# Attention, an ELU layer and a maxout layer on one core: the order of the steps where the second stage hands over to the third and the third to the fourth

## The chip, the cores and the metric

The kernel runs on one core of one Trainium2 chip. The time is the device time of one launch in microseconds (us), the median of three runs. TensorE (PE, with its weight loads as PEld), VectorE (DVE), ScalarE (ACT), GpSimd (POOL) and SyncE (SP, which issues nearly all transfers) each work through their own instruction list in order and wait for each other by semaphores.

## The reference

```python
def reference(q, k, v, w_in, w_out, w1, w2, w3, w_out2):      # names shortened
    x = causal_softmax_attention(q, k, v)      # 2 x 12 heads, 448 tokens, 64 wide
    x = x.transpose(0, 2, 1, 3).reshape(896, 768)
    h = x @ w_in                               # 768 -> 2048
    x = np.where(h > 0, h, np.exp(np.minimum(h, 0)) - 1) @ w_out    # 2048 -> 768, "y" in the kernel
    h = np.maximum(np.maximum(x @ w1, x @ w2), x @ w3)   # 768 -> 768 each
    return h @ w_out2                          # 896 x 768
```

The weights are 64-bit floats, which the kernel turns into 32-bit ones on ScalarE and VectorE. From the second stage on, a product is made of three: each operand is split into a high and a low half, and high x high, high x low and low x high are added up in PSUM.

## The kernel before, in words

**First stage** (to about 99 us): attention, by an order written out by hand, with the first parts of `x @ w_in` in it. **Second stage:** 16 blocks of `x @ w_in` with the ELU, then `g @ w_out` in 24 panels `n` (6 column blocks m, 4 panels each, L700 to L732). The weights of a panel lie in one of three buffers with the tag `ws`, the sums in PSUM banks `py[m, 0]` (512 tokens) and `py[m, 1]` (384). `y_copy(m)` brings them to `y` in SBUF. `y` is kept in two halves of rows (blocks 0 to 2 and 3 to 5) and two halves of tokens `T[0]`, `T[1]`.

**Third stage** (L734 to L1016): the three products `x @ w1, w2, w3` by a scheme with seven products of half-size matrices instead of eight, in nine units n = 0 to 8 (`ITEMS`: column block j, matrix i). The seven left operands are splits of parts and sums of `y`: `a00`, `s3` (made early, in the buffer `x1`), `a01`, `s2`, `s1`, `a11`, `s4` (in the pool `late`, which takes the SBUF of the second stage's `g` tiles). `part(name, k, src)` makes a split: one ScalarE copy and one VectorE subtraction. For each unit the right operands come from a `quad` of weights: `split_first(n)` gives `ws_a` (tag `ws` again), `weight_sums(n)` four sums on VectorE, `split_sums(n)` and `split_last(n)` give `wb`. A call `x1(n)` to `x7(n)` is nine matmuls of 448 columns into one PSUM bank: x1, x6, x7, x4 run on in one bank of kind `bx` (three banks), x2 has one of `bz` (three), x5 and x3 share one of `by` (two). Between them `keep_p`, `keep_u`, `keep_v` copy the running sum out on ScalarE, and the `result...` steps add the copies on VectorE and take the maximum into `h`. The steps stand in the order in which each engine does them (`manual_schedule`): the loop at L956 issues for unit n also x1 and x2 of unit n + 2, and the last two units are written out (L981 to L1016). In the loop `turn_half` turns a half block of `w_out2` from doubles; its load goes into the memory that `y` leaves free.

**Fourth stage** (L1023 to L1140): `h @ w_out2` by the same kind of scheme, on quarters `A[t, k]` of `h` and `Bq[k, n]` of `w_out2`: `quadrant` is one of seven products (27 matmuls of 384 columns into three banks), `rest` the 128 tokens left over. `first` holds the splits for its first product, `token_sums(k)` makes the sums of `h` (in place, and `s3`), `t1` to `t4` those of `w_out2`; `fill` splits 1152 columns a partition into a `slot`, and `p1`, `u`, `v` are running sums in SBUF. The 14 answers of 128 x 384 are added into tiles `o` and sent by SP. The banks go round in the order of `kinds`.

PSUM banks and SBUF buffers are reused in the order in which they are asked for: the first instruction that writes a new tile waits for the last use of the old one there. The eight banks of the second stage become `bx`, `bz` and `by` in the order of their first use; y's last two sums `py[5, 0]` and `py[5, 1]` lie in the first two.

Of the kernel before, what the change touches and what calls it, by code (L numbers as in the profile page):

```python
# [31 lines left out]
def tile_attention_elu_maxout(  # L32
# [28 lines left out]
    def f32(ap):  # L61
        return ap.bitcast(F32)
# [594 lines left out]
    def add(out, x, y, op=ALU.add):  # L657
        nc.vector.tensor_tensor(out, x, y, op)  # L658
# [4 lines left out]
    with tc.manual_schedule():  # L663
# [5 lines left out]
        def part(name, k, src):  # L669
            split(ops[name][:, 0, k], ops[name][:, 1, k], src)  # L670
# [121 lines left out]
        def bank3(kind, n):  # L792
            return ps.tile([P, 512], F32, tag=kind, bufs=BUFS[kind], name=f"{kind}{n}")
# [36 lines left out]
        def result_x(n):  # L830
            o, i = place(n, 1, 0)
            if i == 0:
                copy(o, X.pop(n)[:, :S])
            else:
                add(o, o, X.pop(n)[:, :S], ALU.max)

        split_first(0)
        weight_sums(0)
        split_first(1)
        part("a01", slice(0, 2), y[:, 3:5, T[0]])  # L840
        part("s2", slice(0, 2), y[:, 0:2, T[0]])
        part("s1", slice(0, 2), y[:, 0:2, T[1]])
        part("a11", slice(0, 2), y[:, 3:5, T[1]])
        split_sums(0)
        split_last(0)
        add(y[:, 3:5, T[0]], y[:, 3:5, T[0]], y[:, 0:2, T[0]], ALU.subtract)
        part("s4", slice(0, 2), y[:, 3:5, T[0]])
        y_copy(KD - 1)
        h = late.tile([P, KF2, NT], F32, tag="h", name="h")
        x1(0)  # L850
        x1(1)
        part("a01", 2, y[:, 5, T[0]])
# [5 lines left out]
        x2(0)  # L858
        x2(1)
        part("a11", 2, y[:, 5, T[1]])  # L860
        add(y[:, 5, T[0]], y[:, 5, T[0]], y[:, 2, T[0]], ALU.subtract)
        part("s4", 2, y[:, 5, T[0]])
        result(0, 0, 0, p.pop(0), Z.pop(0))
        result(1, 0, 0, p.pop(1), Z.pop(1))

# [35 lines left out]
        def split_left(k):  # L901
            t = cv.tile([P, 2, K2, P], F32R, tag="c", bufs=2, name=f"left{k}")
            lefts.append(t)
            split(t[:, 0], t[:, 1], h[:, k * K2 : (k + 1) * K2, LEFT])

        def first_tiles():
            for k in range(K2):
                t = cv.tile([P, 2, 2, DMO], F32R, tag="ws", bufs=3, name=f"first{k}")
                first.append(t)

        def first_part(k, x):
            src = (A[0, 0], Bq[0, 0])[x][:, k]
            split(first[k][:, x, 0], first[k][:, x, 1], src)

# [6 lines left out]
        def token_sums(k):  # L921
            s = late.tile([P, S], F32, tag="p", bufs=4, name=f"s3_{k}")[:, :DMO]
            add(s, A[0, 0][:, k], A[1, 0][:, k], ALU.subtract)
            s3.append(s)
            add(A[1, 0][:, k], A[1, 0][:, k], A[1, 1][:, k])
            add(A[0, 0][:, k], A[1, 0][:, k], A[0, 0][:, k], ALU.subtract)

        def last_sums(k):
            add(A[0, 1][:, k], A[0, 1][:, k], A[0, 0][:, k], ALU.subtract)

# [1 line left out]
            product("x6", n, X[n], True)  # L932

        def x5(n):
            Y[n] = bank3("by", n)
            product("x5", n, Y[n], False)

        def x7(n):
# [5 lines left out]
        def x3(n):  # L944
            product("x3", n, Y[n], True)
# [10 lines left out]
        for n in range(NI - 2):  # L956
            x6(n)
            if n > 0:
                result_c01(n - 1)
            if n + 3 < NI:  # L960
                load_quad(n + 3)
            split_first(n + 2)
            x5(n)
            keep_u(n)
            weight_sums(n + 1)
            turn_half()
            x7(n)
# [12 lines left out]

# [6 lines left out]
        split_sums(n + 1)  # L987
        split_last(n + 1)
        x7(n)
        first_tiles()  # L990
        x6(n + 1)
        keep_v(n)
        result_c11(n)
        keep_u(n + 1)
        x4(n)
        for k in range(K2):
            first_part(k, 0)
        result_x(n)
        x3(n)
        for k in range(K2):  # L1000
            first_part(k, 1)
        x7(n + 1)
        result_c01(n)
        keep_v(n + 1)
        x5(n + 1)
        tx = late.tile([P, 3, K2, DMO], F32, tag="wb", bufs=2, name="tx")
        t1, t2, t3 = (tx[:, x] for x in range(3))
        token_sums(0)
        result_c11(n + 1)
        x4(n + 1)  # L1010
        add(t1, Bq[0, 1], Bq[0, 0], ALU.subtract)
        add(t3, Bq[1, 1], Bq[0, 1], ALU.subtract)
        result_x(n + 1)
        x3(n + 1)
        split_left(0)
        token_sums(1)  # L1016
        token_sums(2)
        t = act.tile([P, 2, 2, K2, DMO], F32R, tag="x1", name="slot_x1")
        pair["x7"] = t[:, 0], t[:, 1]
        for k in range(K2):  # L1020
            split(t[:, 0, 0, k], t[:, 0, 1, k], s3[k])

        kinds = ["bz", "bz", "bz", "bx", "bx", "by", "bx", "by"]  # L1023

# [28 lines left out]
        def store(o, row, n):  # L1053
            nc.sync.dma_start(out[row : row + P, n * DMO : (n + 1) * DMO], o)

        def answer(t, tok, n):
            return wk.tile([P, 512], F32, tag=f"mx{n}", name=f"o{tok}_{n}_{t}")[:, :DMO]

        def keep(name):
            t = raw_tile(name, name == "v")  # L1060
            return f32(t.rearrange("p n w -> p (n w)"))[:, : K2 * DMO].rearrange(
                "p (t n) -> p t n", t=K2
            )

        p1, u, v = (keep(x) for x in ("p1", "u", "v"))
        f_a, f_b = (lambda c, k, x=x: first[k][:, x, c] for x in range(2))

        x1 = banks("f1_")
        quadrant(x1, f_a, f_b)
        l1 = bank4("l1")  # L1070
        rest(l1, f_b, 0, True)
        fill(pair["x7"][1], t3)
        result_c01(NI - 1)
        for t in range(K2):
            copy(p1[:, t], x1[t])
        add(t2, Bq[1, 1], t1, ALU.subtract)
        pair["x2"] = slot("a01"), slot("s2")
# [12 lines left out]
        fill(pair["x5"][0], A[1, 0])  # L1090
        fill(pair["x5"][1], t1)
        for t in range(K2):
            o = answer(t, 0, 0)
            add(o, p1[:, t], x2[t])
            store(o, t * P, 0)
        x6 = banks("f6_")
        quadrant(x6, *map(side, pair["x6"]))
        pair["x4"] = pair["x7"]
        fill(pair["x4"][0], A[1, 1])
        o = answer(0, 2, 0)  # L1100
        copy(o, l1)
        store(o, LEFT.start, 0)
        t4 = Bq[1, 0]
        add(t4, t4, t2, ALU.subtract)
        for t in range(K2):
            add(u[:, t], p1[:, t], x6[t])
            add(v[:, t], u[:, t], x7[t])
        fill(pair["x4"][1], t4)
        x5 = banks("f5_")
        quadrant(x5, *map(side, pair["x5"]))  # L1110
        for k in range(K2):
# [2 lines left out]
        fill(pair["x3"][0], A[0, 1])  # L1114
        fill(pair["x3"][1], Bq[1, 1])
        for t in range(K2):
            o = answer(t, 1, 1)
            add(o, v[:, t], x5[t])
            store(o, TOK[1].start + t * P, 1)
            add(u[:, t], u[:, t], x5[t])  # L1120
        x4 = banks("f4_")
        quadrant(x4, *map(side, pair["x4"]))
        b12 = pair["x6"][1]
        fill(b12, Bq[0, 1])
        for t in range(K2):
            o = answer(t, 1, 0)
            add(o, v[:, t], x4[t])
            store(o, TOK[1].start + t * P, 0)
        l2 = bank4("l2")
        rest(l2, side(pair["x3"][1]), 1, True)  # L1130
        x3 = banks("f3_")
        quadrant(x3, *map(side, pair["x3"]))
        rest(l2, side(b12), 0, False)
        for t in range(K2):
            o = answer(t, 0, 1)
            add(o, u[:, t], x3[t])
            store(o, t * P, 1)
        o = answer(0, 2, 1)
        copy(o, l2)
        store(o, LEFT.start, 1)  # L1140


# [34 lines left out]
```

## Time and profile before

| | |
|---|---|
| median of 3 runs | 497.69 us (496.41 to 497.90) |
| profiled execution: time, span | 500.33 us, 498.5 us |
| mean granted TensorE clock | 0.993 of full speed |
| busy share of the span | PE 96%, PEld 84%, DVE 78%, ACT 63%, POOL 10% |
| end of the second stage's last product | 323.9 us |
| third stage's products | 329.75 to 449.1 us |
| fourth stage's products | 449.14 to 493.5 us |

The span is from the first to the last instruction of the profiled execution; its time includes 1.83 us around it. Positions below are us from the span's start. An engine's busy share tells little by itself; what counts is where TensorE stands still, and which work ended that.

### The profile page before, as it was taken

To read this page: it belongs to the slowest core of one execution; us is meant where nothing else is said; L and a number is where in the kernel's file an instruction comes from. 1 tells how busy PE (TensorE), PEld (TensorE's weight loads), DVE (VectorE), ACT (ScalarE), POOL (GpSimd) and SP (SyncE) were. 2 spreads that over 40 slices of the span, in tenths; PEclk is the share of its full clock that TensorE was granted. 3 is DMA by queue.
4 is the path that set the end of the run, shared out by engine and by line. 5 is a ranking of instruction groups with operands and counts; after the bars stand their busy time and mean duration, and the time that the engine had idled before them with its cause. 6 is when DMAs were issued, how large, how long until landed. Compare 5 with 4: busy or idle time off the path is not lost.

```text
span 498.5 us, 7505 instructions
## 1 busy us (share of the span) xinstructions
PE 480.9 (96%) x2677; PEld 418.0 (84%) x2677; DVE 386.9 (78%) x758; ACT 316.1 (63%) x648; POOL 50.5 (10%) x104
## 2 busy tenths in 40 slices
PE   9999999999999999999999999959999999998895
PEld 5776767798999988998899899849999999998795
DVE  3999889679989767767767666768788787689884
ACT  4999899578989867766657555545444443435430
POOL 1664665400000000000000000000000000000000
PEclk9999999999999999999999999979999999999999
DMA  9999310037786554256786676403343430000103
GB/s 187 253 226 200 84 37 2 1 101 251 224 276 202 182 180 141 82 183 218 245 262 210 221 250 227 159 0 128 126 127 124 129 102 27 2 1 1 63 17 142
DMA packets 81509, 69.69 MB, mean 140 GB/s; under 512 B 35136, under 2 KB 75328, under 8 KB 81472
## 3 DMA queue, kind: packets, MB, share of 16 engines
q1 hardware_dynamic: 80544, 68.99, 46.4%
q8 instruction: 21, 0.34, 0.3%
q10 hardware_dynamic: 928, 0.23, 0.2%
q14 instruction: 16, 0.13, 0.1%
HBM read 59.38 MB, written 9.83 MB: 139 GB/s over the span
## 4 chain that ended last, share of the span: by engine, by line
PE 84%; DVE 9%; ACT 3%; POOL 2%; DMA 1%; issue 1%; DVEq 0%; ACTq 0%; POOLq 0%
PE ph L357 23%; PE py L723 22%; PE bx L781 14%; PE by L781 6%; PE s L234 4%; PE te L297 4%; PE bz L781 3%; PE av L322 3%; POOL e L287 2%; ACT e L268 1%; DMA out_dram<-o 1%; DVE h L658 1%; DVE slot_x L138 1%; PE idle L448 1%; PE bzf L1035 1%; PE tk L196 1%
## 5 line engine op out<-in xcount | busy, mean ns | idle before, releaser
L357 PE MATMUL ph<-x,ws_l 128*128 128x512 f32 (+2 forms) x576 | 118.7, 365 | 0.0
L723 PE MATMUL py<-gs,ws_o 128*128 128x512 f32 (+1 forms) x576 | 116.2, 363 | 0.0
L357 PEld LDWEIGHTS ph<-x,ws_l 128*128 128x128 f32 x576 | 103.8, 188 | 12.5 <-issue 1.0
L723 PEld LDWEIGHTS py<-gs,ws_o 128*128 128x128 f32 x576 | 104.3, 188 | 11.7
L287 POOL TENSOR_SCALAR e<-e,r 112x336 f32<-112x336 f32 (+3 forms) x96 | 49.1, 532 | 42.6 <-DVE r L281 41.9
L268 ACT ACTIVATE e<-e,nm 112x448 f32<-112x448 f32 (+3 forms) x96 | 49.7, 528 | 3.3 <-DVE nm L254 3.1
L254 DVE CUSTOM_DVE_ANT_0 e<-s,mask 112x224 f32<-112x224 f32 (+3 forms) x96 | 37.9, 441 | 3.2 <-PE s L234 3.0
L781 PE MATMUL by<-ops_s,wb 128*128 128x448 f32 x162 | 36.4, 368 | 0.0
L137 ACT ACTIVATE ws_o<-c_o 128x512 fp32r<-128x512 f32 x24 | 15.1, 631 | 32.2 <-PE py L723 30.7
L781 PEld LDWEIGHTS by<-ops_s,wb 128*128 128x128 f32 x162 | 30.4, 188 | 3.1
L297 PE MATMUL te<-ident,e 112*112 112x112 f32 x240 | 27.7, 261 | 1.5 <-POOL e L287 1.2
L138 DVE TENSOR_TENSOR ws_o<-c_o,ws_o 128x512 fp32r<-128x512 f32 x24 | 16.6, 691 | 15.8 <-ACT ws_o L137 15.8
L661 ACT ACTIVATE u<-bx 128x448 f32<-128x448 f32 x9 | 4.9, 546 | 36.0 <-PE bx L781 36.0
L297 PEld LDWEIGHTS te<-ident,e 112*112 112x112 f32 x240 | 23.8, 133 | 4.4 <-POOL e L287 2.8
L781 PE MATMUL bx<-ops_a_s,ws_a 128*128 128x448 f32 x81 | 20.2, 401 | 5.8 <-ACT y L661 5.8
L234 PE MATMUL s<-qk 64*112 64x224 f32 (+3 forms) x192 | 24.9, 405 | 0.0
L322 PE MATMUL av<-et,vn 112*64 112x448 f32 (+3 forms) x192 | 24.4, 403 | 0.0
L138 DVE TENSOR_TENSOR gs<-g,gs 128x512 fp32r<-128x512 f32 (+2 forms) x30 | 18.7, 622 | 6.9 <-ACT gs L137 6.7
L99 DVE SCALAR_TENSOR_TENSOR ce<-ce,raw_e 128x768 uint32<-128x768 uint32 x18 | 17.2, 958 | 8.6 <-ACT raw_e L95 8.5
L781 PEld LDWEIGHTS bx<-ops_a_s,ws_a 128*128 128x128 f32 x81 | 16.9, 211 | 8.0 <-ACT y L661 6.2
L99 DVE SCALAR_TENSOR_TENSOR c_o<-c_o,raw_o 128x512 uint32<-128x512 uint32 x24 | 16.6, 692 | 8.8 <-ACT raw_o L95 7.4
L137 ACT ACTIVATE gs<-g 128x512 fp32r<-128x512 f32 (+2 forms) x30 | 17.2, 574 | 8.7 <-DVE g L373 8.7
(167 smaller groups left out, 867.5 us busy)
## 6 DMA issues: line engine op xcount, KB each, us to landing
raw_e<-in_moe_w_dram SPq DMA_DIRECT2D x18, 768.0 KB, 4.9
raw_l<-in_moe_w_in_dram SPq DMA_DIRECT2D x16, 768.0 KB, 4.8
raw_o<-in_moe_w_out_dram SPq DMA_DIRECT2D x24, 512.0 KB, 3.5
turned<-ce SPq DMA_DIRECT2D x18, 384.0 KB, 2.7
quad<-turned SPq DMA_DIRECT2D x18, 384.0 KB, 4.3
wx<-in_moe_w_out_dram SPq DMA_DIRECT2D x12, 384.0 KB, 3.1
qn<-in_q_dram SPq DMA_DIRECT2D x24, 112.0 KB, 3.8
vn<-in_v_dram SPq DMA_DIRECT2D x12, 224.0 KB, 3.7
```

What stands on the lines that cost most here:

```text
L99: nc.vector.scalar_tensor_tensor(r, r, 3, low, ALU.logical_shift_left, ALU.bitwise_or)
L137: nc.scalar.activation(hi, src, AF.Copy)
L138: nc.vector.tensor_tensor(lo, src, f32(hi), ALU.subtract)
L234: nc.tensor.matmul(s[j][:C, o : o + (c + 1) * C], qk[:, a, c * C : (c + 1) * C], qk[:, c2, : (c + 1) * C], start=(w == 0 and n == 0), stop ...
L254: nc.vector.tensor_tensor_reduce(out=e_t[h][:, EOFF[c] : EOFF[c] + (c + 1) * C], in0=ps_now.pop(("s", h, c)), in1=mask[:, (NCH - 1 - c) * ...
L268: nc.scalar.activation(e, e, AF.Exp, bias=nm_t[h][:, c : c + 1], scale=-1.0, accum_out=sm_t[p][:, j, c : c + 1],)
L287: nc.gpsimd.tensor_scalar(e, e, ps_now["r", h][:, c : c + 1], 1.0, ALU.mult, ALU.mult)
L297: nc.tensor.transpose(t[:C, n : n + C], e[:, EOFF[c] + j * C : EOFF[c] + (j + 1) * C], ident[:C, :C],)
L322: nc.tensor.matmul(a[j * D : (j + 1) * D, kc * C : S], vn[:, j * NCH + kc, :], et[j][:, TOFF[kc] : TOFF[kc] + S - kc * C], start=(n == 0), ...
L357: nc.tensor.matmul(ps, w(a, kc), x(c, kc), start=(i == 0), stop=(i == len(seq) - 1))
L723: nc.tensor.matmul(py[m, b][:, : at.stop - at.start], w[:, a, kc * P : (kc + 1) * P], g_sp[hk * HK + kc][:, c, at], start=(hk == 0 and i = ...
L781: nc.tensor.matmul(bank[:, :S], w, side[:, c, k, :], start=(not onto and k == 0 and (a, c) == (0, 0)), stop=(k == K2 - 1 and (a, c) == (1, ...
```

## The change

- **Second to third stage.** `weight_sums(0)` goes ahead of `split_first(0)`, and `split_first(1)` behind the first four `part` steps. The subtraction that forms the operand `s4`, and its split, are no longer made for rows 3 and 4 ahead of `y_copy(5)` and for row 5 behind x2(1), but once for all three rows, behind x2(1). The bank of x5(0), kind `by`, is asked for ahead of the banks of x1.
- **Last three units.** `t1`, four of the six `first_part` steps and `token_sums(0)` move up into the loop's last pass (n = 6), between `result_x(6)` and x3(6). The other two `first_part`, `token_sums(1)`, `t3` and the splits of `s3` move up by some steps each among units 7 and 8. `t1` and `t3` lie in buffers of the tags `raw` and `apart` in place of one tile `tx`, `t2` is made later.
- **Answers.** The 14 answers go round over eight buffers (`mx0`, `p`, `mx1`, `p`: two, four, two) in place of two and two. `t4` and the copy of `l1` move, and the two fills for x4 stand among the `u`, `v` sums in place of around them.

```diff
@@ second to third stage
+        weight_sums(0)
         split_first(0)
-        weight_sums(0)
-        split_first(1)
         part("a01", slice(0, 2), y[:, 3:5, T[0]])
         part("s2", slice(0, 2), y[:, 0:2, T[0]])
         part("s1", slice(0, 2), y[:, 0:2, T[1]])
         part("a11", slice(0, 2), y[:, 3:5, T[1]])
+        split_first(1)
         split_sums(0)
         split_last(0)
-        add(y[:, 3:5, T[0]], y[:, 3:5, T[0]], y[:, 0:2, T[0]], ALU.subtract)
-        part("s4", slice(0, 2), y[:, 3:5, T[0]])
         y_copy(KD - 1)
         h = late.tile([P, KF2, NT], F32, tag="h", name="h")
+        Y[0] = bank3("by", 0)
         x1(0)
         x1(1)
...
         part("a11", 2, y[:, 5, T[1]])
-        add(y[:, 5, T[0]], y[:, 5, T[0]], y[:, 2, T[0]], ALU.subtract)
-        part("s4", 2, y[:, 5, T[0]])
+        add(y[:, 3:6, T[0]], y[:, 3:6, T[0]], y[:, 0:3, T[0]], ALU.subtract)
+        part("s4", slice(0, 3), y[:, 3:6, T[0]])
@@ the loop over units, and the last two units
             result_x(n)
+            if n == NI - 3:
+                t1 = keep("t1")
+                add(t1, Bq[0, 1], Bq[0, 0], ALU.subtract)
+                for k in range(K2 - 1):
+                    first_part(k, 0)
+                    first_part(k, 1)
+                token_sums(0)
             x3(n)
...
         x4(n)
-        for k in range(K2):
-            first_part(k, 0)
+        first_part(K2 - 1, 0)
+        first_part(K2 - 1, 1)
         result_x(n)
         x3(n)
-        for k in range(K2):
-            first_part(k, 1)
+        token_sums(1)
         x7(n + 1)
         result_c01(n)
         keep_v(n + 1)
         x5(n + 1)
-        tx = late.tile([P, 3, K2, DMO], F32, tag="wb", bufs=2, name="tx")
-        t1, t2, t3 = (tx[:, x] for x in range(3))
-        token_sums(0)
+        t3 = keep("t3", True)
+        add(t3, Bq[1, 1], Bq[0, 1], ALU.subtract)
         result_c11(n + 1)
         x4(n + 1)
-        add(t1, Bq[0, 1], Bq[0, 0], ALU.subtract)
-        add(t3, Bq[1, 1], Bq[0, 1], ALU.subtract)
+        t = act.tile([P, 2, 2, K2, DMO], F32R, tag="x1", name="slot_x1")
+        pair["x7"] = t[:, 0], t[:, 1]
+        for k in range(K2 - 1):
+            split(t[:, 0, 0, k], t[:, 0, 1, k], s3[k])
         result_x(n + 1)
         x3(n + 1)
+        token_sums(2)
+        split(t[:, 0, 0, 2], t[:, 0, 1, 2], s3[2])
+        fill(pair["x7"][1], t3)
         split_left(0)
-        token_sums(1)
-        token_sums(2)
-        t = act.tile([P, 2, 2, K2, DMO], F32R, tag="x1", name="slot_x1")
-        pair["x7"] = t[:, 0], t[:, 1]
-        for k in range(K2):
-            split(t[:, 0, 0, k], t[:, 0, 1, k], s3[k])
@@ fourth stage
-        def answer(t, tok, n):
-            return wk.tile([P, 512], F32, tag=f"mx{n}", name=f"o{tok}_{n}_{t}")[:, :DMO]
+        homes = ["mx0", "p", "mx1", "p"]
+        def answer(name):
+            homes.append(homes.pop(0))
+            if homes[-1] == "p":
+                return late.tile([P, S], F32, tag="p", bufs=4, name=name)[:, :DMO]
+            return wk.tile([P, 512], F32, tag=homes[-1], name=name)[:, :DMO]
...
+        t4 = Bq[1, 0]
+        add(t4, t4, t2, ALU.subtract)
         x6 = banks("f6_")
         quadrant(x6, *map(side, pair["x6"]))
         pair["x4"] = pair["x7"]
-        fill(pair["x4"][0], A[1, 1])
-        o = answer(0, 2, 0)
-        copy(o, l1)
-        store(o, LEFT.start, 0)
-        t4 = Bq[1, 0]
-        add(t4, t4, t2, ALU.subtract)
+        reply(LEFT.start, 0, l1)
         for t in range(K2):
             add(u[:, t], p1[:, t], x6[t])
             add(v[:, t], u[:, t], x7[t])
-        fill(pair["x4"][1], t4)
+            if t < 2:
+                fill(pair["x4"][t], (A[1, 1], t4)[t])
```

## Rows read from the trace of the kernel before

**Rows 1.** Waits of TensorE from 300 us on: total, times, longest

```profile
PE bx L781 <- ACT y L661: 5.8, 1, 5.8
PE bxf L1035 <- DVE slot_x L138: 1.5, 1, 1.5
PE bxf L1035 <- DVE v L658: 1.3, 1, 1.3
PE bxf L1035 <- ACT o L661: 1.1, 1, 1.1
```

**Rows 2.** Windows: stretch, length, busy time by engine, granted clock, DMA

```profile
324.00:329.70 5.70, 0.00 (x0) 0.00 (x0) 4.68 (x7) 2.70 (x6) 0.00 (x0) 0.82 0.00 0
329.70:334.00 4.30, 4.25 (x11) 3.80 (x12) 3.05 (x5) 1.91 (x6) 0.00 (x0) 0.50 0.00 0
...
470.00:476.00 6.00, 3.58 (x20) 3.06 (x19) 5.13 (x7) 1.65 (x2) 0.00 (x0) 1.00 0.21 77
```

**Rows 3.** Timeline, second to third stage: start, length, engine, line, operation, idle before

```profile
314.30 0.85 ACT L137 ACTIVATE ws_a<-quad 128x768 fp32r<-128x768 f32 x1 [1.82 <-PE py L723]
...
319.18 0.85 ACT L137 ACTIVATE ws_a<-quad 128x768 fp32r<-128x768 f32 x1 [4.03 <-PE py L723]
319.93 0.94 ACT L137 ACTIVATE ops_a<-y 128x896 fp32r<-128x896 f32 x1
...
327.14 1.09 DVE L658 TENSOR_TENSOR y<-y 128x896 f32<-128x896 f32 x1
328.27 0.95 ACT L137 ACTIVATE ops_s<-y 128x896 fp32r<-128x896 f32 x1 [3.00 <-DVE y L658]
329.12 0.96 ACT L661 ACTIVATE y<-py 128x512 f32<-128x512 f32 x2
...
329.75 6.09 PE L781 MATMUL bx<-ops_a_s,ws_a 128*128 128x448 f32 x18 [5.82 <-ACT y L661]
...
335.68 3.88 PE L781 MATMUL bz<-ops_a,ws_a 128*128 128x448 f32 x18
...
339.43 0.33 SPq L875 DMA_DIRECT2D wx<-in_moe_w_out_dram  x1
...
342.74 0.56 ACT L94 ACTIVATE wx<-wx 128x384 f32<-128x384 f32 x1 [0.73 <-DMA wx<-in_moe_w_out_dram]
...
344.98 1.20 PE L781 MATMUL bx<-ops_a_s,ws_a 128*128 128x448 f32 x5
```

**Rows 4.** Lines by form, VectorE from 440 and ScalarE from 310 us

```profile
L658 DVE TENSOR_TENSOR h<-h 128x384 f32<-128x384 f32 x9 | 4.8, 555 | 0.2
...
L658 DVE TENSOR_TENSOR tx<-wx 128x1152 f32<-128x1152 f32 x2 | 2.6, 1352 | 0.0
...
L137 ACT ACTIVATE ops_s<-y 128x448 fp32r<-128x448 f32 x3 | 1.7, 574 | 3.1 <-DVE y L658 3.1
```

**Rows 5.** Timeline, end of the third stage (units 6 to 8)

```profile
428.95 0.62 DVE L658 TENSOR_TENSOR r<-p,bz 128x448 f32<-128x448 f32 x1 [2.04 <-PE bz L781]
...
431.27 1.02 DVE L658 TENSOR_TENSOR c_t<-quad 128x384 f32<-128x384 f32 x2
...
433.73 1.58 ACT L137 ACTIVATE wb<-c_t 128x768 fp32r<-128x768 f32 x2 [0.58 <-DVE c_t L658]
...
434.61 1.83 DVE L138 TENSOR_TENSOR wb<-c_t,wb 128x768 fp32r<-128x768 f32 x2 [1.25 <-ACT wb L137]
...
436.12 2.02 PE L781 MATMUL bx<-ops_s,wb 128*128 128x448 f32 x9
```

**Rows 6.** Timeline, fourth stage: its first product, its last, the last answers

```profile
449.14 4.85 PE L1035 MATMUL bzf<-first 128*128 128x384 f32 x27
...
491.74 1.73 PE L1035 MATMUL bxl<-slot_a,left 128*128 128x384 f32 x9
...
494.49 0.55 DVE L658 TENSOR_TENSOR o<-u,bxf 128x384 f32<-128x384 f32 x1 [1.65 <-DMA out_dram<-o]
495.04 0.49 ACT L661 ACTIVATE o<-bxl 128x384 f32<-128x384 f32 x1 [11.51 <-DVE o L658]
```

More of the change, by code (lines that the diff above doesn't have):

```diff
@@ L904, in split_left, with first_part @@
             split(t[:, 0], t[:, 1], h[:, k * K2 : (k + 1) * K2, LEFT])
-        def first_tiles():
-            for k in range(K2):
+        def first_part(k, x):
+            if k == len(first):
                 t = cv.tile([P, 2, 2, DMO], F32R, tag="ws", bufs=3, name=f"first{k}")
                 first.append(t)
-        def first_part(k, x):
             src = (A[0, 0], Bq[0, 0])[x][:, k]
@@ L926, in token_sums, with keep @@
             add(A[0, 0][:, k], A[1, 0][:, k], A[0, 0][:, k], ALU.subtract)
+        def keep(name, apart=False):
+            t = f32(raw_tile(name, apart).rearrange("p n w -> p (n w)"))
+            return t[:, : K2 * DMO].rearrange("p (k n) -> p k n", k=K2)
         def last_sums(k):
@@ L934, in x5 @@
         def x5(n):
-            Y[n] = bank3("by", n)
+            if n not in Y:
+                Y[n] = bank3("by", n)
             product("x5", n, Y[n], False)
@@ L989, in tile_attention_elu_maxout @@
         x7(n)
-        first_tiles()
         x6(n + 1)
@@ L1005, in tile_attention_elu_maxout @@
         x5(n + 1)
-        tx = late.tile([P, 3, K2, DMO], F32, tag="wb", bufs=2, name="tx")
-        t1, t2, t3 = (tx[:, x] for x in range(3))
-        token_sums(0)
+        t3 = keep("t3", True)
+        add(t3, Bq[1, 1], Bq[0, 1], ALU.subtract)
         result_c11(n + 1)
         x4(n + 1)
-        add(t1, Bq[0, 1], Bq[0, 0], ALU.subtract)
-        add(t3, Bq[1, 1], Bq[0, 1], ALU.subtract)
+        t = act.tile([P, 2, 2, K2, DMO], F32R, tag="x1", name="slot_x1")
+        pair["x7"] = t[:, 0], t[:, 1]
+        for k in range(K2 - 1):
+            split(t[:, 0, 0, k], t[:, 0, 1, k], s3[k])
         result_x(n + 1)
         x3(n + 1)
+        token_sums(2)
+        split(t[:, 0, 0, 2], t[:, 0, 1, 2], s3[2])
+        fill(pair["x7"][1], t3)
         split_left(0)
-        token_sums(1)
-        token_sums(2)
-        t = act.tile([P, 2, 2, K2, DMO], F32R, tag="x1", name="slot_x1")
-        pair["x7"] = t[:, 0], t[:, 1]
-        for k in range(K2):
-            split(t[:, 0, 0, k], t[:, 0, 1, k], s3[k])
         kinds = ["bz", "bz", "bz", "bx", "bx", "by", "bx", "by"]
@@ L1054, in store, with reply @@
             nc.sync.dma_start(out[row : row + P, n * DMO : (n + 1) * DMO], o)
-        def answer(t, tok, n):
-            return wk.tile([P, 512], F32, tag=f"mx{n}", name=f"o{tok}_{n}_{t}")[:, :DMO]
[L1059 to L1065, printed above, removed]
-        f_a, f_b = (lambda c, k, x=x: first[k][:, x, c] for x in range(2))
+        homes = ["mx0", "p", "mx1", "p"]
[4 more added lines that the diff above has]
+            return wk.tile([P, 512], F32, tag=homes[-1], name=name)[:, :DMO]
+        p1, u, v = (keep(x, x == "v") for x in ("p1", "u", "v"))
+        f_a, f_b = (lambda c, k, x=x: first[k][:, x, c] for x in range(2))
+        def reply(row, n, x, y=None):
+            o = answer(f"o{row}_{n}")
+            if y is None:
+                copy(o, x)
+            else:
+                add(o, x, y)
+            store(o, row, n)
         x1 = banks("f1_")
@@ L1071, in tile_attention_elu_maxout @@
         rest(l1, f_b, 0, True)
-        fill(pair["x7"][1], t3)
         result_c01(NI - 1)
@@ L1075, in tile_attention_elu_maxout @@
             copy(p1[:, t], x1[t])
-        add(t2, Bq[1, 1], t1, ALU.subtract)
         pair["x2"] = slot("a01"), slot("s2")
@@ L1080, in tile_attention_elu_maxout @@
         split_left(1)
+        t2 = late.tile([P, K2, DMO], F32, tag="wb", bufs=2, name="t2")
+        add(t2, Bq[1, 1], t1, ALU.subtract)
         x7 = banks("f7_")
@@ L1092, in tile_attention_elu_maxout @@
         for t in range(K2):
-            o = answer(t, 0, 0)
-            add(o, p1[:, t], x2[t])
-            store(o, t * P, 0)
+            reply(t * P, 0, p1[:, t], x2[t])
+        t4 = Bq[1, 0]
+        add(t4, t4, t2, ALU.subtract)
         x6 = banks("f6_")
@@ L1116, in tile_attention_elu_maxout @@
         for t in range(K2):
-            o = answer(t, 1, 1)
-            add(o, v[:, t], x5[t])
-            store(o, TOK[1].start + t * P, 1)
+            reply(TOK[1].start + t * P, 1, v[:, t], x5[t])
             add(u[:, t], u[:, t], x5[t])
@@ L1125, in tile_attention_elu_maxout @@
         for t in range(K2):
-            o = answer(t, 1, 0)
-            add(o, v[:, t], x4[t])
-            store(o, TOK[1].start + t * P, 0)
+            reply(TOK[1].start + t * P, 0, v[:, t], x4[t])
         l2 = bank4("l2")
@@ L1134, in tile_attention_elu_maxout @@
         for t in range(K2):
[L1135 to L1140, printed above, removed]
+            reply(t * P, 1, u[:, t], x3[t])
+        reply(LEFT.start, 1, l2)
 _INS = [
```

## The prediction, made before the changed kernel ran

> **What bounds the kernel now.** TensorE is busy for nearly the whole span, so I read first the list of what TensorE waited for in the stretch that the change touches [rows 1]. It has four entries of weight: one of 5.8 us where the third stage begins, ended by a ScalarE copy of `y`, and three of 1.1 to 1.5 us in the fourth stage. Nothing stands there for the 90 us between: units 0 to 8 run without a wait. From x1(2) at 344.98 [rows 3] to x6(8) at 436.12 [rows 5] lie 49 chains of nine matmuls, so a chain takes 91.14 / 49 = 1.86 us.
>
> The windows then say what the long wait costs beyond itself [rows 2]. TensorE does nothing from 324.0 to 329.7, and the mean granted clock falls to 0.82 there; in the next 4.3 us it is 0.50, the lower of the two levels (1.2 GHz), and later 1.00 again. In the fourth stage TensorE stands for 2.4 of the 6 us from 470 to 476, in pieces, and the clock stays at 1.00.
>
> The timeline at the handover shows why TensorE stood [rows 3]. The last product of `y` ends at 329.75 - 5.82 = 323.93. ScalarE had waited until 319.18 with `split_first(1)`, whose buffer was in use, and everything behind it on ScalarE waited too. The operand splits followed one after another, then the `y` subtraction for `s4` on VectorE (327.14 to 328.23), then its split, and only at 329.12 the copies of the last two `y` banks. x1(0) needed one of those banks.
>
> In the fourth stage, 24 groups of nine matmuls lie between 449.14 and 491.74 [rows 6]. 27 matmuls take 4.85 and nine take 1.73, so a group in a row takes 3.12 / 2 = 1.56, and 24 take 37.44. The other 42.60 - 37.44 = 5.16 us TensorE stood still. After its last group began, the last answer started only 3.30 us later (495.04), though the group takes 1.73: answers before it had waited for stores to free their two buffers (1.65 at 494.49).
>
> **The change, part by part.** I walk each engine through its new order with the durations of the rows, on the clock of the trace of before.
>
> *Handover, gain.* Without `split_first(1)` ahead of them, the four splits run on ScalarE from 314.30 + 0.85 on, at about 0.85 each, until 318.5; `split_first(1)` then still starts at 319.18, and its VectorE part ends near 322.4, ahead of x1(1) at 325.6. ScalarE is free at about 321.9, so the `y` copies start when the last product ends. x1(0) no longer needs those banks: the first two now go to x5(0) and x5(1), 9 us later. So x1 follows the last product directly. A matmul's recorded end lies 0.2 us past the start of its follower, so x1(0) starts at 323.74 in place of 329.75: 6.01 us. The 18 matmuls of x1(0) and x1(1) took 6.09 us after the standstill, and the 18 of x2 took 3.88: 2.21 us more come back when the clock has no reason to fall. Together 8.22 us.
>
> *Handover, what it costs.* The work on row 5 of `y` still hangs on the copies, and now lies beside running products. From 323.93: copies 0.96, split of `a01` 0.57 and 0.62, `y_sums` 2 x 0.62, split of `s2` 0.57 and 0.62: 328.5 (durations from [rows 3 to 5], 448-wide 0.57 on ScalarE and 0.62 on VectorE). x2(0) is due at 323.74 + 2 x 1.86 = 327.46 and needs only `a01` (326.1); x6(0) is due at 331.2. Splits of `s1` and `a11`, with a `keep_p` copy each on ScalarE, take about 0.92 each: 330.4. Then the subtraction over 1344 columns, which the trace doesn't have: between 1.09 (896) and twice that; 1.35 for 1152 [rows 4] puts it at 1.56. Its split is 1.33 on ScalarE (0.95 for 896) and 1.56 on VectorE, and VectorE stands during the first: 334.8. Behind it on VectorE wait three result steps (1.75) and the VectorE part of `split_first(2)` (0.95): 337.4. x1(2) is due at 323.74 + 7 x 1.86 = 336.76 and waits 0.69. Bounds: nothing if the chain is 0.7 shorter, 1.7 if it is 1 us longer.
>
> The first load of a `w_out2` half goes out when `y` has been read: 339.43 before, now 334.9. ScalarE waited for it until 342.74, 3.31 after issue; now until 338.2. Its two ops (about 1.0) and `keep_v(0)` behind them end at 339.75, while x4(0) is due at 337.45 + 1.86 = 339.31: 0.49 more (nothing to 1.0). All the later steps of units 0 and 1 come out with over 2 us to spare. Handover in sum: 8.22 - 0.69 - 0.49 = 7.04 us.
>
> *Last units.* VectorE takes on `t1` (1.35), four `first` parts and three sums (7 x 0.555) ahead of `result_c00(8)`: 5.2 us, some 4.9 with the usual overlap of neighbours. Before, it stood idle for 2.04 there [rows 5], so the results start 2.8 later; 0.7 of this is made up in front of `weight_sums(8)`, which ends 2.1 later. Its first split ended at 434.61 + 0.95 = 435.56 before, and x6(8) started at 436.12 with 0.56 to spare. Now x6(8) waits 1.5; ScalarE had idled 0.58 ahead of this split, 0.35 of it past the recorded end of the sums, and if that vanishes the wait is 1.2. I take 1.45 (0 to 2.1). From there each step that the list issues is due before TensorE wants it, by my walk: x3(7), x7(8), x5(8), x3(8) (0.3 and more to spare). The steps moved are VectorE and ScalarE work; no transfer moves with them.
>
> *Fourth stage.* Everything is now on the clock + 1.45: x1 starts at 450.6, x7 is due at 456.84 and its operands are ready at 453.4 (the wait of 1.5 goes); x2 is due at 461.5 with operands at 459.7; x6 at 467.8 with operands at 464. The copy of `l1` no longer waits for a buffer and ends at 468.45, ahead of the second bank of x6 (469.3; the wait of 1.1 goes). VectorE runs three answers from 466.45, `t4` (1.35) to 469.2, and then the pairs u, v (0.55 each) with the fills for x4 (1.35 each) between: the pairs end at 470.66, 472.98 and 475.30. The third bank of x6 (470.9) is free in time. The first two banks of x5 are due at 472.4 and 474.6 and wait for the second and third pair: 0.60 + 0.75. After this VectorE is ahead. Standing still 1.35 in place of 5.16: 3.81 gained (from 2.3, if the waits stay as long as the old 1.1 and 1.3 and one more, to 5.16).
>
> *Answers.* With eight buffers each is used again eight answers later. The last answer follows the last group: 1.76 after its start in place of 3.30, 1.54 gained. The store behind it costs what it did (498.5 - 495.53 = 2.97).
>
> *Sum:* 7.04 - 1.45 + 3.81 + 1.54 = 10.94 us. The span becomes 487.6, the profiled execution's time 489.4. The median of the runs lies 2.64 below that time; I take the gain from the median: 497.69 - 10.9 = 486.8 us.
>
> **The rivals.** *Splits that start late.* `a01` to `a11` lie where `g` tiles lay. The trace has their first split at 319.93, while the products of `y` ran on to 323.93, so they don't wait for all of them; but ScalarE was blocked until 319.18 by another wait, so the row can't say that they were free at 315. If they are free only at 319.2, the chain of row 5 comes 1.8 later, and x1(2) with it: 488.6 us. Chance 0.08.
>
> *The banks don't change hands* (this part does nothing). Then x1(0) waits for the first copy, 0.8 us; but 0.7 of it was waited at x1(2) anyway: 487 us. Speaking against: x1 waited for the copy of `y`, so the first kind asked for has the first banks. It lies inside the forecast.
>
> *The clock falls in the new gaps* (1.45 at x6(8), 1.35 in x5). At 2.21 each as at the handover: 491.2 us. Against it: from 470 to 476 TensorE stood as much, at 1.00. The Trainium skill (TensorE: Matmul & The Clock Gate, A second HAM failure mode: psum-queue depth-cycling) tells of short standstills between groups that cycle through PSUM banks and made the clock go back and forth; by that rule this kernel's fourth stage should show it already, and its rows do not. Chance 0.04.
>
> *Fewer waits.* If the chains on VectorE are a little shorter than walked, the waits at x1(2), x4(0), x6(8) and x5 (together 3.98) shrink; with all gone 482.8. Chance of ending below 484.5: 0.08.
>
> *VectorE becomes the bound of the end, and the kernel slower.* From unit 6 to x5 VectorE now hardly rests, and each us that its chain grows, for work or waits that I overlooked, is one us of TensorE. To be slower by 0.3% (1.5 us, about what a measurement of this kernel can tell from no change) it must grow by 12.4 us; to be level with before, by 10.9. Between 426 and 484 that is a fifth of its work. Nothing in the rows comes near; no wait of VectorE there is over 2.1. Chance 0.02, 500 us and more; within 0.3%, 0.02. A smaller growth of 4 to 9 us (491 to 496 us): 0.04.
>
> **How the numbers follow.** The forecast of 486.8 with its bounds has 0.72. Bounds: the unknown at the handover 7 - 1 to 7 + 1.2, x6(8) -0.7 to +1.45, x5 and its neighbours +-1.4; not all to one side, so some +-2.5. The range 484.5 to 490.5 holds nearly all of this and the late splits, 0.80 in all; left out are fewer waits (0.08), the clock (0.04) and what lies above. Faster 0.96, within 0.3% 0.02, slower 0.02.
>
> **What would show it.** Right: in the windows of the handover no standstill and a granted clock of 1.00; the list of TensorE's waits has, in place of the 5.8, short ones at x1(2) and x4(0), one of about 1.5 at x6(8), and in the fourth stage only the two in x5; no answer waits for a store. The `y` copies start within 0.1 us of the last product's end, and the four splits run between 315 and 319. Wrong: splits that start at 319 (late buffers), x1(0) released by a `y` copy (banks), a window of the last units at 0.5 (clock), or waits of TensorE for VectorE over 2 us in units 7 and 8.

## The result, and the profile after

The changed kernel takes 486.17 us (median of 4 runs, 484.97 to 486.54), the kernel before 497.31 us (4 runs, 496.41 to 497.90): a ratio of 0.9773, 95% interval 0.9749 to 0.9798, so 11.1 us less (10.0 to 12.5). The profiled execution took 485.87 us with a span of 484.1.

The list of TensorE's waits from 290 us on, in the changed kernel (total, times, longest), stands against [rows 1]:

```profile
PE bx L781 <- ACT v L661: 0.5, 1, 0.5
PE bx L781 <- ACT wb L137: 0.4, 1, 0.4
PE bx L781 <- DVE wb L138: 0.3, 1, 0.3
PE bx L781 <- DVE ws_a L138: 0.3, 1, 0.3
```

The 5.8 us are gone, and so is every wait in the fourth stage. Four short ones remain, all in the third stage. The windows of the changed kernel (columns as in [rows 2]) show the handover, its next 10 us, the rest of the third stage and the fourth:

```profile
324.00:330.00 6.00, 6.00 (x32) 5.55 (x31) 3.31 (x7) 3.82 (x8) 0.00 (x0) 1.00 0.00 0
330.00:340.00 10.00, 9.18 (x44) 7.85 (x43) 8.50 (x13) 4.25 (x7) 0.00 (x0) 1.00 0.36 118
340.00:438.00 98.00, 97.31 (x479) 89.53 (x479) 82.85 (x138) 46.05 (x86) 0.00 (x0) 1.00 0.27 85
438.00:480.40 42.40, 42.40 (x243) 42.01 (x241) 36.72 (x51) 16.09 (x19) 0.00 (x0) 1.00 0.16 57
```

TensorE is busy in all of 324 to 330, where it had stood still, the granted clock is 1.00 throughout, and in the fourth stage it is busy all the time. The timeline of the handover in the changed kernel answers to [rows 3]:

```profile
315.15 0.93 ACT L137 ACTIVATE ops_a<-y 128x896 fp32r<-128x896 f32 x1
...
319.22 0.85 ACT L137 ACTIVATE ws_a<-quad 128x768 fp32r<-128x768 f32 x1 [0.61 <-PE py L723]
...
323.87 3.81 PE L781 MATMUL bx<-ops_a_s,ws_a 128*128 128x448 f32 x18
324.06 0.98 ACT L661 ACTIVATE y<-py 128x512 f32<-128x512 f32 x2 [2.11 <-PE py L723]
...
327.51 3.81 PE L781 MATMUL bz<-ops_a,ws_a 128*128 128x448 f32 x18
...
330.35 1.55 DVE L658 TENSOR_TENSOR y<-y 128x1344 f32<-128x1344 f32 x1
...
333.29 1.56 DVE L138 TENSOR_TENSOR ops_s<-y,ops_s 128x1344 fp32r<-128x1344 f32 x1 [1.40 <-ACT ops_s L137]
...
334.92 0.33 SPq L874 DMA_DIRECT2D wx<-in_moe_w_out_dram  x1
...
336.49 0.95 DVE L138 TENSOR_TENSOR ws_a<-quad,ws_a 128x768 fp32r<-128x768 f32 x1
336.63 0.57 PE L781 MATMUL bx<-ops_a_s,ws_a 128*128 128x448 f32 x2
...
337.49 1.70 PE L781 MATMUL bx<-ops_a_s,ws_a 128*128 128x448 f32 x7 [0.29 <-DVE ws_a L138]
...
339.72 2.09 PE L781 MATMUL bx<-ops_a,wb 128*128 128x448 f32 x9 [0.53 <-ACT v L661]
```

The splits begin at 315.15, behind nothing but `split_first(0)`. The `y` copies start when the last product ends, and x1(0) starts 0.19 us before them. The row-5 chain runs beside products and ends at 334.85. x1(2) starts when it is due but stops after two of its nine matmuls until VectorE has written the low half. x4(0) at 339.72 is the last of the handover to wait, behind the turned half of `w_out2` whose load went out at 334.92. The end of the third stage in the changed kernel, against [rows 5]:

```profile
418.34 1.35 DVE L658 TENSOR_TENSOR t<-wx 128x1152 f32<-128x1152 f32 x1
...
423.13 0.61 DVE L658 TENSOR_TENSOR r<-p,bz 128x448 f32<-128x448 f32 x1
...
425.55 1.99 PE L781 MATMUL bx<-ops_a_s,wb 128*128 128x448 f32 x9
...
427.92 0.68 PE L781 MATMUL bx<-ops_s,wb 128*128 128x448 f32 x2 [0.38 <-ACT wb L137]
...
428.92 1.69 PE L781 MATMUL bx<-ops_s,wb 128*128 128x448 f32 x7 [0.31 <-DVE wb L138]
...
430.44 1.78 PE L781 MATMUL bx<-ops_a,wb 128*128 128x448 f32 x8
```

VectorE's new steps fill 418.34 to 423.13, and x6(8) waits twice, for either half of its right operand. Last, the fourth stage of the changed kernel, against [rows 6]:

```profile
441.38 4.87 PE L1040 MATMUL bzf<-first 128*128 128x384 f32 x27
...
457.28 0.55 DVE L658 TENSOR_TENSOR o<-p,byf 128x384 f32<-128x384 f32 x1
...
463.24 0.55 DVE L658 TENSOR_TENSOR v<-u,byf 128x384 f32<-128x384 f32 x1
463.26 1.72 PE L1040 MATMUL byf<-slot_wb,slot_s 128*128 128x384 f32 x9
...
464.82 1.72 PE L1040 MATMUL bxf<-slot_wb,slot_s 128*128 128x384 f32 x9
...
465.56 0.55 DVE L658 TENSOR_TENSOR v<-u,bxf 128x384 f32<-128x384 f32 x1
...
478.87 1.73 PE L1040 MATMUL bxl<-slot_a,left 128*128 128x384 f32 x9
...
480.63 0.49 ACT L661 ACTIVATE o<-bxl 128x384 f32<-128x384 f32 x1 [9.74 <-PE bxl L1040]
```

From the first product to the last group lie 478.87 - 441.38 = 37.49 us, the 24 x 1.56 of a stage without a gap (42.60 before), and the last answer starts 1.76 after the last group.

**Against which execution.** The two profiled spans differ by 14.4 us, 3.3 more than the medians. The kernel before was therefore profiled twice more (`before_p2`, `before_p3` below): its spans in all runs go from 494.5 to 498.6. `before_p2`, with 495.0, has the chain of nine matmuls at 1.825 us that the changed kernel has (1.86 in the first profile). Set out from the moment at which y's last product would hand over (322.79 there, 323.87 after), it takes 172.21 us to the end, the changed kernel 160.23. These 11.98 us are what the steps below divide up. The handover in `before_p2`:

```profile
328.79 5.70 PE L781 MATMUL bx<-ops_a_s,ws_a 128*128 128x448 f32 x18 [5.82 <-ACT y L661]
334.33 3.81 PE L781 MATMUL bz<-ops_a,ws_a 128*128 128x448 f32 x18
```

### The profile page after: what moved, and what is told of

Same layout as the page of the kernel before. It is cut to its first block, busy times and chain, and to the rows that moved or that the text cites. A ratio compares the mean times of both kernels' runs of the same rounds, so it can differ in the third digit from the quotient of the medians.

```text
span 484.1 us, 7498 instructions
## 1 busy us (share of the span) xinstructions
PE 476.4 (98%) x2677; PEld 416.2 (86%) x2677; DVE 386.0 (80%) x756; ACT 315.6 (65%) x647; POOL 50.4 (10%) x104
## 4 chain that ended last, share of the span: by engine, by line
PE 87%; DVE 5%; ACT 4%; POOL 2%; DMA 1%; issue 0%; POOLq 0%; ACTq 0%; DVEq 0%; SPq 0%
PE py L723 24%; PE ph L357 23%; PE bx L781 10%; PE by L781 6%; PE s L234 4%; PE te L297 4%; PE av L322 3%; PE bzf L1040 3%; PE bz L781 2%; PE bxf L1040 2%; POOL e L287 2%; PE byf L1040 2%; PE bxl L1040 1%; ACT e L268 1%; PE idle L448 1%; PE tk L196 1%
## 5 line engine op out<-in xcount | busy, mean ns | idle before, releaser
L357 PEld LDWEIGHTS ph<-x,ws_l 128*128 128x128 f32 x576 | 103.8, 188 | 12.5 <-issue 1.0
L322 PEld LDWEIGHTS av<-et,vn 112*64 112x64 f32 x192 | 11.9, 137 | 12.5 <-issue 5.6
L234 PEld LDWEIGHTS s<-qk 64*112 64x112 f32 x192 | 16.0, 173 | 6.7 <-issue 2.0
```

The costliest lines, as they stand in the source:

```text
L234: nc.tensor.matmul(s[j][:C, o : o + (c + 1) * C], qk[:, a, c * C : (c + 1) * C], qk[:, c2, : (c + 1) * C], start=(w == 0 and n == 0), stop ...
L322: nc.tensor.matmul(a[j * D : (j + 1) * D, kc * C : S], vn[:, j * NCH + kc, :], et[j][:, TOFF[kc] : TOFF[kc] + S - kc * C], start=(n == 0), ...
L357: nc.tensor.matmul(ps, w(a, kc), x(c, kc), start=(i == 0), stop=(i == len(seq) - 1))
```

## The experiments

Each is compared with the kernel before on the same chip: experiments 1, 2, 4 and 7 on one chip, where its median is 497.05 us (17 runs), 3, 5, 6 and `best` on a second (497.56, 13 runs), `best2` and experiment 8 on a third (497.46, 11 runs).

**1. The kernel before against itself** (`before_again`, no edit).

> The kernel before, unchanged, for the time of one chain of nine 448-column matmuls. In the first profile it was 1.86 us, in the changed kernel's 1.825. If that rate belongs to the execution or the chip, it may come out at 1.83 here. If it belongs to the order of the PSUM banks, it is 1.86 again. Time: ratio 1.000.

497.47 us, ratio 0.9991 (0.9969 to 1.0014). So 0.3% is what such a comparison can tell.

**2. The handover alone** (`handover_only`): the kernel before with the new order at the handover and the early bank; the last units and the fourth stage as before.

```diff
+        weight_sums(0)
         split_first(0)
-        weight_sums(0)
-        split_first(1)
...
+        split_first(1)
...
-        part("s4", slice(0, 2), y[:, 3:5, T[0]])
...
+        Y[0] = bank3("by", 0)
...
+        part("s4", slice(0, 3), y[:, 3:6, T[0]])
...
```

> Only the new order at the handover from the second to the third stage and x5's bank asked for first; the last units and the fourth stage as before. If the terms of the forecast add up, 7.0 us faster (490.3 us, ratio 0.986), with 0.4 to 0.5 us waits at x1(2) and x4(0) and none at x6(8), and the three waits of the fourth stage (1.5, 1.1, 1.3) as before. If part of the gain there is given back later to VectorE, under 5 us.

490.68 us, ratio 0.9844 (0.9811 to 0.9877): 6.4 us by the medians. Its profile gives 165.62 us from x1(0) at 323.38 to the end at 489.0, 6.6 less than 172.21. x1(2) and x4(0) wait as in the whole change; the fourth stage waits 1.6, 1.3 and 1.1 us as before, and x6(8) not at all.

**3. The rest alone** (`old_handover`): the changed kernel with the handover of before, the same lines the other way round.

> The changed kernel with the handover of before: what the last units, the fourth stage and the answers give alone. By the trace of the changed kernel 1.24 us lost at x6(8), 5.16 gained in the fourth stage and 1.54 at the end: 5.4 us faster, ratio 0.989; the gains of this and of handover_only then add up to that of the whole change (11 us). With the standstill of 5.8 us back, the chain of nine is 1.86 again if the standstill sets it, 1.825 if anything in the last units or the fourth stage does.

492.27 us, ratio 0.989 (0.9866 to 0.9914): 5.3 us. The wait of 5.8 is back, x6(8) waits 0.4 and 0.3, the fourth stage never. Its windows around the handover:

```profile
324.00:328.00 4.00, 0.00 (x0) 0.00 (x0) 4.00 (x5) 1.08 (x2) 0.00 (x0) 0.93 0.00 0
328.00:332.00 4.00, 2.44 (x7) 2.18 (x8) 2.71 (x5) 2.28 (x4) 0.00 (x0) 0.50 0.00 0
332.00:336.00 4.00, 4.00 (x16) 3.60 (x15) 1.47 (x3) 1.92 (x4) 0.00 (x0) 0.72 0.00 0
```

The two halves add up within the noise: 0.9844 x 0.989 = 0.9736, by the two intervals about 0.970 to 0.978, against 0.9773 (0.9749 to 0.9798) for the whole. These runs show no sign that one half leans on the other.

**4. Without the early bank** (`no_bank`): the changed kernel less one line.

```diff
-        Y[0] = bank3("by", 0)
```

> The changed kernel without the early request of x5's bank, so that x1(0) and x1(1) take the first two banks again. My walk: x1(0) starts behind the first copy of y, 0.8 us later, but most of that was waited at x1(2) anyway, so 0.2 to 0.5 us slower than the changed kernel (ratio to the kernel before 0.978). Rival: the clock falls or the chain of row 5 comes later too, over 1.5 us slower than the changed kernel. On the chain of nine matmuls: 1.86 us if the rate belongs to the banks, else as in the changed kernel.

485.25 us, ratio 0.9737 (0.9704 to 0.9769): no slower than the whole change. TensorE's timeline in it:

```profile
324.56 3.91 PE L781 MATMUL bx<-ops_a_s,ws_a 128*128 128x448 f32 x18 [0.69 <-ACT y L661]
...
337.43 1.99 PE L781 MATMUL bx<-ops_a_s,ws_a 128*128 128x448 f32 x9
339.52 2.09 PE L781 MATMUL bx<-ops_a,wb 128*128 128x448 f32 x9
```

x1(0) now waits for a `y` copy, but x1(2) runs without a stop, and x4(0), due at 337.43 + 1.825 = 339.26, is 0.26 late. It starts 15.61 us after the `y` copies began (323.91); in the changed kernel it is 15.66 (324.06 to 339.72). The same work decides in both, and from the first `y` copy to the end they take 159.99 and 160.04 us.

**5. The early bank alone** (`bank_only`): the kernel before with that line (and x5 taking the bank that is there).

```diff
+        Y[0] = bank3("by", 0)
         x1(0)
...
-            Y[n] = bank3("by", n)
+            if n not in Y:
+                Y[n] = bank3("by", n)
```

> The kernel before with only x5's bank asked for first. x1(0) and x1(1) then follow the last product of y directly, and TensorE stands still later, ahead of x2(0), whose operand is ready at 331.2 as before: 3.6 us in place of 5.8. x2(0) starts 4.4 us earlier, and x1(2) waits about 1.0 for its weights: 3.4 us faster, ratio 0.993. If the clock falls in this gap too, 2.2 less: 0.9975. If a standstill with no fall of the clock slows the chains, they are 1.86 here at a clock of 1.00.

494.37 us, ratio 0.993 (0.9906 to 0.9955). TensorE's timeline, and then its windows:

```profile
322.67 3.81 PE L781 MATMUL bx<-ops_a_s,ws_a 128*128 128x448 f32 x18
326.32 1.38 PE L781 MATMUL bz<-ops_a,ws_a 128*128 128x448 f32 x6
329.50 0.47 PE L781 MATMUL bz<-ops_a,ws_a 128*128 128x448 f32 x1 [1.80 <-ACT ops_a L137]
```

```profile
324.00:328.00 4.00, 3.70 (x19) 3.08 (x17) 3.13 (x4) 1.00 (x2) 0.00 (x0) 1.00 0.00 0
328.00:332.00 4.00, 2.31 (x10) 1.88 (x11) 2.94 (x5) 2.11 (x6) 0.00 (x0) 1.00 0.00 0
```

The standstill moves behind 24 matmuls and breaks into pieces (1.8, 0.2, 0.4 and 0.4), and the clock stays at 1.00. The expectation had one stop of 3.6 ahead of x2(0), but six matmuls of x2(0) run before they need row 5. This profile is of the fastest of six runs (492.74 us); the mean clocks of the others go from 0.994 to 1.00, so it may have fallen in some of them. In the old order the line is worth 3 us; in the new order, by experiment 4, nothing that can be measured.

**6. The clock by itself** (`warm_before`): the kernel before, with x1(0) computed three times more into the bank of x2(0), which x2(0) then overwrites. These 27 matmuls are extra work in the standstill.

```diff
...
+        X[0] = bank3("bx", 0)
+        Z[0] = bank3("bz", 0)
+        for _ in range(3):
+            product("x1", 0, Z[0], False)
         x1(0)
```

> The kernel before, with 27 more matmuls in the gap at the handover: the product x1(0) three times into the bank that x2(0) then overwrites. TensorE has something to do from 323.9 to about 329.5, and the rest of the order is that of before. Clock alone: the granted clock stays at 1.00, x1(0) and x1(1) take 3.72 in place of 5.9 us, 2.2 us faster (ratio 0.9956), the chain of nine stays 1.86. If the standstill or the low clock also sets the rate of the chains behind it, they come at 1.825 and 63 of them give 2.2 us more: 4.4 us faster, ratio 0.991.

495.10 us, ratio 0.9951 (0.9934 to 0.9968): more work, and 2.5 us less. TensorE's timeline in it:

```profile
322.82 5.63 PE L781 MATMUL bz<-ops_a_s,ws_a 128*128 128x448 f32 x27
328.80 3.92 PE L781 MATMUL bx<-ops_a_s,ws_a 128*128 128x448 f32 x18 [0.35 <-ACT y L661]
332.56 3.81 PE L781 MATMUL bz<-ops_a,ws_a 128*128 128x448 f32 x18
```

The real work starts at 328.80, no earlier than in `before_p2` (328.79), but its 18 matmuls take 3.76 in place of 5.54, at a granted clock of 1.00. The chains behind them come at 1.825, which the expectation took for a sign that the standstill or the low clock sets their rate. It is none by itself: `before_p2`, with the standstill, has 1.825 too (experiment 8).

**7. Two answer buffers each** (`old_answers`): the changed kernel with four answer buffers in place of eight.

```diff
...
-            homes.append(homes.pop(0))
-            if homes[-1] == "p":
-                return late.tile([P, S], F32, tag="p", bufs=4, name=name)[:, :DMO]
-            return wk.tile([P, 512], F32, tag=homes[-1], name=name)[:, :DMO]
+            return wk.tile([P, 512], F32, tag=f"mx{name[-1]}", name=name)[:, :DMO]
```

> The changed kernel with the answers over two and two buffers as before. If the buffers held what the forecast says: 1.5 us more at the end (last answer 3.3 us after the start of the last group) and up to 1.1 us more where the copy of l1 waits for a store and the second bank of x6 for that copy; 487.7 to 489 us, ratio 0.981 to 0.983. Rival: with the answers spread out by the new order, two buffers are enough, and the ratio stays 0.977.

487.83 us, ratio 0.979 (0.9757 to 0.9823), 2.6 us above `no_bank` on the same chip. The timeline of its fourth stage:

```profile
457.87 1.72 PE L1040 MATMUL bzf<-slot_a,slot_s 128*128 128x384 f32 x9
459.16 0.56 DVE L658 TENSOR_TENSOR o<-p,bzf 128x384 f32<-128x384 f32 x1 [1.56 <-DMA out_dram<-o]
...
460.21 3.73 PE L1040 MATMUL bxf<-slot_a,slot_s 128*128 128x384 f32 x18 [0.61 <-ACT o L661]
...
463.78 1.72 PE L1040 MATMUL byf<-slot_wb,slot_s 128*128 128x384 f32 x9
...
482.95 0.49 ACT L661 ACTIVATE o<-bxl 128x384 f32<-128x384 f32 x1 [11.49 <-DVE o L658]
```

An answer waits for a store; the copy of `l1`, which frees a bank, is behind it, and x6 behind that: three groups take 463.78 - 457.87 = 5.91 where 3 x 1.56 = 4.68 would do. At the end the last answer starts 3.57 after the last group (479.38) in place of 1.76. So the buffers are worth 1.23 + 1.81 = 3.04 us in the profile: they serve x6 as well as the end.

**8. Two more profiles of the kernel before** (`before_p2`, `before_p3`, no edit).

> The kernel before, unchanged, profiled a third time. Its executions lie between spans of 494.5 and 498.6; the two profiled so far (498.5, 497.6) lie high and have chains of nine at 1.86. If the rate of the chains belongs to the execution, a profile with a span near 495 shows 1.825; if it belongs to this program, any profile of it shows 1.86 whatever its span.

> The same a fourth time: 1.825 with a span near 495, or 1.86 with one of 497 to 498.6, if rate and span go together.

Spans 495.0 and 496.7. Two successive chains in `before_again` (span 497.6), then in `before_p2`:

```profile
338.50 2.02 PE L781 MATMUL bx<-ops_s,wb 128*128 128x448 f32 x9
340.36 2.02 PE L781 MATMUL by<-ops_s,wb 128*128 128x448 f32 x9
```

```profile
337.97 1.99 PE L781 MATMUL bx<-ops_s,wb 128*128 128x448 f32 x9
339.80 1.99 PE L781 MATMUL by<-ops_s,wb 128*128 128x448 f32 x9
```

1.86 and 1.83 us apart: one program, two rates. `before_p3` has 1.825 too, with a longer slow stretch after the standstill (x1(0) and x1(1) in 6.03 us against 5.54). Neither the order of the banks nor the standstill fixes the rate: `no_bank`, with the old bank order, and `old_handover`, with the old standstill, have 1.825. But a link with the standstill isn't excluded. Of the five profiles with the 5.8 us two have 1.86; the seven in which nothing near it is left at the handover (the changed kernel, `handover_only`, `no_bank`, `warm_before`, `old_answers`, `best`, `best2`) all have 1.825, and so has `bank_only`, whose stops are 1.8 us and shorter. And where the kernel before goes from 496.27 to 499.26 us in 13 runs, `warm_before` on the same chip goes from 494.94 to 495.91 in eight.

**9. The waits that were left** (`best`): the changed kernel with the results of units 0 and 1 behind `split_first(2)`, the first `turn_half` behind `keep_v(0)`, and `t1` with one first part ahead of `result_c11(6)`, where VectorE has room. `best2` moves all four first parts there.

```diff
-        result(0, 0, 0, p.pop(0), Z.pop(0))
-        result(1, 0, 0, p.pop(1), Z.pop(1))
@@ the loop
             split_first(n + 2)
+            if n == 0:
+                result(0, 0, 0, p.pop(0), Z.pop(0))
+                result(1, 0, 0, p.pop(1), Z.pop(1))
             x5(n)
             keep_u(n)
             weight_sums(n + 1)
-            turn_half()
+            if n > 0:
+                turn_half()
+            if n == NI - 3:
+                t1 = keep("t1")
+                add(t1, Bq[0, 1], Bq[0, 0], ALU.subtract)
+                first_part(0, 1)
...
             keep_v(n)
+            if n == 0:
+                turn_half()
...
```

> The changed kernel with the three waits left in its third stage taken up: the results of units 0 and 1 go behind the split of unit 2's weights, unit 0's first half block of w_out2 behind keep_v(0), and t1 with one of the first parts into VectorE's idle 1.9 us ahead of result_c11(6). Each wait then goes (0.45 at x1(2), 0.53 at x4(0), 1.24 at x6(8)): 2.2 us faster than the changed kernel, 484.0 us, ratio 0.973 or a little under. Rival: VectorE is the bound there, and what is taken from one wait comes back at the next; then under 1 us.

> The version best with all four early first parts ahead of result_c11(6), so that only token_sums(0) is left between result_x(6) and result_c00(8). The last wait of its third stage (0.5 at x6(8)) goes: no entry of the list of TensorE's waits from 290 us on, 0.5 us faster than best, ratio to the kernel before about 0.970. Rival: result_c11(6) comes 1.3 later by this, and the splits of unit 7 behind it hold up x6(7); then not faster.

`best`: 482.79 us, ratio 0.9707 (0.9682 to 0.9732). `best2`: 482.88 us, ratio 0.9694 (0.9667 to 0.9722). TensorE's waits from 290 us on in `best` are one row, and in `best2` none:

```profile
PE bx L781 <- DVE wb L138: 0.3, 1, 0.3
```

From x1(0) to the end they take 158.21 and 157.59 us, against 160.23: 2.0 us less in `best`, where 2.2 were expected. The times can't tell the two apart.

## Why the prediction was right, step by step

The forecast was 486.8 us with 484.5 to 490.5; measured 486.17. Its terms against `before_p2`, both profiles taken at 1.825 a chain:

| step | predicted, us | measured, us | worked out from |
|---|---|---|---|
| standstill | +6.01 | +6.00 | 5.82, and x1(0) 0.18 ahead of the recorded end (324.05) |
| clock | +2.21 | +1.90 | 18 matmuls in 5.54, then 327.51 - 323.87 |
| x1(2) | -0.69 | -0.45 | third matmul due at 337.04, started 337.49 |
| x4(0) | -0.49 | -0.81 | due at 337.49 + 7 x 0.203 = 338.91, started 339.72 |
| x6(8) | -1.45 | -1.24 | x4(7) due at 425.55 + 2 x 1.825 = 429.20, started 430.44 |
| fourth stage | +3.81 | +5.18 | 42.67 (445.59 to 488.26), then 37.49 |
| answers | +1.54 | +1.51 | from last group to end: 6.74, then 5.23 |
| sum | +10.94 | +12.09 | 11.98 by the two ends |

**Right.** Where TensorE had stood still, and for how long: `handover_only` takes the long wait away by itself, and `old_handover` brings it back. The row-5 chain, walked engine by engine, ended at 334.85 where 334.8 was forecast, and ScalarE's work ahead of x4(0) was forecast to end at 339.75 for a start at 339.72. The subtraction over 1344 columns, which no row of before had, took 1.55 (1.56 estimated). The steps of units 0 and 1 behind these came out in time.

**Clock, right in kind.** `warm_before` gives it back alone, 1.78 us by its profile against `before_p2` and 2.5 by the runs. The slow stretch of before differs between executions (5.54, 5.68, 5.93 and 6.03 for the 18 matmuls in four profiles), and in some of them its chains are slower as well. 2.21 was the stretch of one execution.

**x1(2), a size.** The step let all nine matmuls wait for VectorE's low half; the trace shows that the first two need only the high half. What x1(2) saved, x4(0) then waited: 1.18 forecast for the two together, 1.26 measured.

**"The first two banks of x5 are due at 472.4 and 474.6 and wait for the second and third pair": wrong.** It took the banks in turn, as the section on the kernel says that they are reused in the order in which they are asked for. There are two of kind `by`; the trace has VectorE reading x7's from 463.24 to 463.79, while x5's first group writes a `by` bank from 463.26. So x5 got the other one, that of x2, which was asked for later but read out earlier (at 457.28 in the same timeline). Its second group, of kind `bx`, starts at 464.82, while x7's `bx` bank next in turn is read only from 465.56; it too got another. In turn, x5 would have waited until 463.79 and then until 466.11, which comes to 0.53 + 0.76 = 1.29 us: the walk of VectorE was right, and the rule for the banks was not. Without these waits the fourth stage gives 5.18 in place of 3.81. This is the one term that failed by more than the run of an execution. It failed towards a shorter time, but not for the reason of the rival of fewer waits, which was shorter chains on VectorE.

**"x1(0) no longer needs those banks": true, and worth nothing here.** x1(0) does follow directly, but `no_bank`, which is the rival's case, is no slower: x4(0) hangs on work that begins with the `y` copies either way. Its 0.7 us at x1(0) and a time inside the forecast came out as the rival had them. That the line is worth 3 us in the old order (`bank_only`) shows that its worth depends on what stands behind it.

**The other rivals.** Splits that start late: refuted by 315.15. A clock that falls in the new gaps: refuted, 1.00 in every window, and in the profile of `bank_only` over 1.8 us of standstill too. The rule of the Trainium skill (TensorE: Matmul & The Clock Gate, A second HAM failure mode: psum-queue depth-cycling), by which short standstills between groups that cycle through PSUM banks make the clock go back and forth, shows in none of these profiles: from 342 us to the last matmul each has 1.00. VectorE as the bound of the end: its new work does set x6(8), and `best` removes nearly all of that by putting some of the new steps earlier, where VectorE had room; beyond this it bounds nothing, as the fourth stage has no wait.

**Why the median shows a little less than the sum.** 11.1 us (10.0 to 12.5) against 12.0. The two profiles are one execution each, and y's last product alone ends between 322.8 and 324.1 us from execution to execution; the runs of before may also differ in the rate of their chains, as its profiles do. The difference isn't resolved. That the median came within 0.7 us of the forecast is therefore partly luck: the steps sum to 1.15 us more than forecast, nearly all of it from the banks of x5, and most of that doesn't show in the medians.

## What to carry to other kernels

Walk each engine's list in its new order with measured durations, from the event that releases it to the next time TensorE is due: a start that comes earlier is worth only what the next late operand leaves of it. A buffer that waits for a store can hold up a product through a chain of copies, so look for such buffers before the last answers too. Do not assume that buffers of one kind go round in turn: see in the trace which last reader a new writer overlaps.

## What the runs showed of the hardware

- The same instructions of the same program ran at 1.86 us for nine matmuls of 448 columns in two profiles of the kernel before and at 1.825 in two others, all at a granted clock of 1.00 in these stretches. Over the 56 chains between x1(2) and the fourth stage that is 2 us. What sets the rate stays open: the order of the banks and the standstill don't fix it, but 1.86 was seen only in profiles with the standstill (experiment 8).
- A standstill of 5.8 us brought the granted clock to 0.50, the lower of the two levels, for the products that followed; 1.8 us of standstill followed by shorter ones left it at 1.00 in the one profile taken (`bank_only`). Lengths between these were not tried.
- Filling a standstill with 27 matmuls that nobody needs made the kernel 0.5% faster (experiment 6).
